# Which free slot a load takes: the one that has been free longest, in place of the lowest number

## The chip, the core and the metric

The kernel runs on one core of one Trainium2 chip. The metric is the device time of one execution in microseconds (us); lower is better. All data is in the chip's main memory (HBM) at the start and the result goes back there. The core has a matrix engine (PE, whose weight loads are listed apart as PEld), a vector engine (DVE), a scalar engine (ACT), GpSimd (POOL) and a sync engine (SP), which here issues all the kernel's transfers, one after another, in the order in which the program was written. Sixteen DMA engines carry the transfers out. Engines run unsynchronized and wait for one another on semaphores.

## The reference

Two layers of one-token decoding for a batch of eight, each an attention block over a key and value cache and a small mixer and feed-forward block. Both layers read the same weights and the same caches:

```
x = x + A(layernorm(x))      # attention, pass 1
x = x + B(layernorm(x))      # mixer + MLP
x = x + A(layernorm(x))      # attention, pass 2
x = x + B(layernorm(x))

A:  q = x @ wq                                  # D = 448, 16 query heads of 256
    scores = q . k_cache * 256**-0.5            # 8 kv heads, 4096 keys, Dh = 256
    out = (softmax(scores) @ v_cache) @ wo
B:  h = gelu(layernorm(x) @ w1); four shifted quarters of h; x1 = x + hs @ w2
    out = x1 + gelu(layernorm(x1) @ w3) @ w4
```

The sequence has one position, so every shift in B moves in zeros: the mixer's term vanishes, and w1 and w2 are never read. The caches are bfloat16: 8 batches x 8 kv heads x 4096 keys x 256, 2 MB for the keys and 2 MB for the values of one head of one batch. The values are read twice (once in each pass); most keys are read once and kept on the core between the passes, as told below.

## The kernel before

**Slots.** The on-core buffer for the caches is one array, `slab`, cut into `N_SLOTS = 31` slots of 512 KB (L480 and the lines before it hold their bookkeeping). A slot holds a quarter of one head's keys or values. Slots x and x+1 with even x are mates: a quarter and the next one of the same head can be loaded with a single 1 MB transfer into two mates ("a pair"); otherwise each quarter is a 512 KB transfer ("a single"). Slot 30 has no mate.

**Units and steps.** A unit is one kv head of one batch in one pass: `(p, b, g)`. The main loop goes over the units in a list, four steps for each unit, one for each quarter. In a step it calls `transposes` (DVE turns a raw quarter of the keys, 32 x 32 blocks, from the slot that it was loaded into, into another slot), `k_part` (PE: the scores of that quarter, L653) and one or more `v_part` (PE: probabilities times a quarter of the values, L630, some six steps later than the scores). When pass 1 of a batch is complete (`ends`), the small dense work follows on PE and DVE, spread over the steps up to `fence`: layer norms, the MLP and the next query. In that stretch PE also works through two heads of other batches so as not to stand still.

**What lives how long.** A slot with values is free after its `v_part`. A slot with raw keys is free after its two transposes (L562). A slot with transposed keys is free after `k_part` in pass 2; in pass 1 it stays occupied until pass 2 for six of the eight heads of a batch (`KEEP = 6`), two quarters of which are parked in PSUM instead. So by the end of pass 1 of a batch 22 of the 31 slots hold kept keys, and nine are left for everything in flight.

**The planner.** Which transfer goes into which slot is decided when the program is written, not on the chip: `free` is a Python list, to which a slot's number is appended by the code that writes its last reader. Each time something is freed, `pump` writes as many of the next loads as the list allows, and SP later waits, at each of them, until the slot's last reader has really finished. One slot is held back (`RESERVE = 1`), so that `transposes` always finds a destination. `take` gives a single slot: it prefers those whose mate isn't free, and of these the lowest number. `take_two` gives the lowest two free mates. Pairs are used only outside the dense stretches (`calm`), where loads are marked `wide`; where they are also `firm`, and seven or more quarters are under way, `pump` rather waits for two mates than write two singles. The planner's order of the loads themselves (`loads`), and the order of the work on PE, is fixed beforehand and does not look at slots.

Of the kernel before, what the change touches and what calls it, by code (L numbers as in the profile page):

```python
# [31 lines left out]
def kernel(  # L32
# [340 lines left out]
    lone = {b: [(1, b + 2, g) for g in loose] for b in range(4)}  # L373
# [102 lines left out]
    free = list(range(N_SLOTS))  # L476
# [3 lines left out]
    def take():  # L480

        lone = [x for x in free if x ^ 1 not in free]
        x = min(lone or free)
        free.remove(x)
        return x

    def take_two():

        both = [x for x in free if x % 2 == 0 and x + 1 in free]
        if both:  # L490
            free.remove(both[0])
            free.remove(both[0] + 1)
        return both[:1]
# [16 lines left out]
    def pump():  # L510
        while loads and len(free) > RESERVE:
            kind, t, i = loads[-1]
            _, b, g = units[t]
            if kind == "p":
                loads.pop()
                x = take()
                dst = slots[x].rearrange("p (e q c x) -> p q c e x", e=4, q=2, c=4)
                for j in range(2):
                    src = park[parked[g, i]][j][:].bitcast(BF16)
                    nc.scalar.copy(dst[:, j], src.rearrange("p (c e x) -> p c e x", c=4, e=4))  # L520
                kt_of[(1, b, g), i] = x
                continue
            cache, of = (A_k_cache, raw_of) if kind == "k" else (A_v_cache, v_of)
            n, two = 1, (kind, t, i + 1)
            if i % 2 == 0 and two in wide and two in loads[-PAIR_VIEW:]:
                x = take_two() if len(free) > RESERVE + 1 else []
                if x:
                    n, x = 2, x[0]
                    loads.remove(two)
                elif under_way[0] >= ENOUGH and two in firm:  # L530
                    return
            loads.pop()
            if n == 1:
                x = take()
# [14 lines left out]
    def transposes(i):  # L549


        while len(parts) - len(todo) < by[i]:
            t, s = todo[-1]
            if 4 * t + s > i and ((t, s) not in raw_of or not free):
                return
            todo.pop()
            raw = raw_of.pop((t, s))
            kt = kt_of[units[t], s] = take()
            src = slots[raw].bitcast(FP32).rearrange("p (q c e i) -> p q c e i", q=2, c=4, e=4)
            dst = slots[kt].bitcast(FP32).rearrange("p (e q c r) -> p q c e r", e=4, q=2, c=4)  # L560
            for q in range(2):
                nc.vector.transpose(dst[:, q], src[:, q])  # L562
            _, b, g = units[t]
            if (g, s) in parked:
                for q in range(2):
                    dst = park[parked[g, s]][q][:].rearrange("p (c e r) -> p c e r", c=4, e=4)
                    nc.vector.transpose(dst, src[:, q])
            free.append(raw)
            under_way[0] -= 1
            pump()  # L570
# [377 lines left out]
```

## Time and profile before

| | |
|---|---|
| median of three runs | 1114.25 us (1113.67 to 1115.25) |
| the profiled execution | 1115.99 us, of which 1114.2 us is the span from its first to its last instruction |
| busy share | PE 62%, PEld 58%, DVE 49%, ACT 27%, POOL 9% |
| moved by the DMA engines | 449.77 MB, mean 404 GB/s |
| loads into slots | 227 of 1024 KB, 378 of 512 KB |

The table says how long each engine was at work, not what the end waited for. A busy share is an average over stages with different limits: 62% of PE says nothing of the stretch in which PE is the one that holds up the rest. The rate of the DMA engines in a stretch is the measure that all stretches have in common here, since the bytes are nearly all of the same kind, loads into slots.

### The profile page before, as it was taken

What the parts mean: (1) busy time and instruction counts of PE and PEld (TensorE: products, weight loads), DVE (VectorE), ACT (ScalarE), POOL (GpSimd) and SP (SyncE); (2) the same over time, 40 slices, a digit from 0 to 9 for tenths busy, and PEclk for the clock granted to TensorE, in tenths of its full rate; (3) what the DMA queues carried; (4) which work ended last, traced back from release to release, by engine and by line L of the source; (5) the groups of instructions that cost most, each with busy time, mean ns of one, the idle gap of its engine ahead of it and who ended that gap; (6) DMA issues with size and microseconds to landing.
All of it is one profiled execution on the core that took longest, in us unless ns stands there. A gap on an engine that the chain in (4) does not pass through costs nothing.

```text
span 1114.2 us, 46349 instructions
## 1 busy us (share of the span) xinstructions
PE 687.9 (62%) x20737; PEld 640.8 (58%) x20737; DVE 550.7 (49%) x1305; ACT 306.0 (27%) x1360; POOL 104.1 (9%) x156
## 2 busy tenths in 40 slices
PE   3345675666756576565756667565756667665766
PEld 2334565565646565565655556565656566555765
DVE  4347554654446445554455535563446535554322
ACT  1112124321233212422243212422143212422242
POOL 0001001110011100110011000110011000100011
DMA  9999999999999999999999999999999999999993
GB/s 367 394 418 425 408 417 422 424 417 395 417 423 424 400 403 419 423 424 391 414 420 424 402 410 404 420 424 415 383 421 424 409 412 404 422 423 400 371 405 128
DMA packets 94503, 449.77 MB, mean 404 GB/s; under 512 B 9936, under 2 KB 15968, under 8 KB 64864
## 3 DMA queue, kind: packets, MB, share of 16 engines
q1 hardware_dynamic: 94304, 446.81, 98.4%
q8 instruction: 162, 2.65, 0.9%
q14 instruction: 37, 0.30, 0.1%
HBM read 446.77 MB, written 0.01 MB: 401 GB/s over the span
## 4 chain that ended last, share of the span: by engine, by line
DMA 39%; PE 15%; issue 6%; ACT 6%; DVE 5%; POOL 0%; SPq 0%; DVEq 0%; ACTq 0%; POOLq 0%
DMA slab<-in_A_v_cache_dram 31%; DMA slab<-in_A_k_cache_dram 9%; PE bank L630 5%; PE bank L653 4%; DVE slab L562 3%; ACT pt L720 2%; PE bank L137 1%; ACT slab L520 1%; ACT pe L689 1%; DVE small L686 1%; PE bank L676 1%; PE bank L712 1%; ACT pt_far L720 1%; PE bank L702 1%; PE bank L313 1%
## 5 line engine op out<-in xcount | busy, mean ns | idle before, releaser
L562 DVE STREAM_TRANSPOSE slab<-slab 128x512 f32<-128x512 f32 x640 | 414.6, 687 | 214.7 <-DMA slab<-in_A_k_cache_dram 167.2
L630 PEld LDWEIGHTS <-slab 128*128 128x128 bf16 x8192 | 273.1, 106 | 286.5 <-DMA slab<-in_A_v_cache_dram 223.0
L630 PE MATMUL bank<-pt,slab 128*128 128x2 bf16 x7168 | 260.5, 166 | 232.7 <-DMA slab<-in_A_v_cache_dram 161.5
L653 PE MATMUL bank<-Qblk,slab 128*128 128x8 bf16 x8192 | 297.2, 168 | 77.4 <-DVE slab L562 39.1
L653 PEld LDWEIGHTS <-slab 128*128 128x128 bf16 x8192 | 267.8, 105 | 88.2 <-DVE slab L562 46.6
L689 ACT ACTIVATE pe<-bank,small 128x32 bf16<-128x32 f32 x256 | 61.3, 295 | 406.7 <-DVE small L686 406.7
L731 POOL TENSOR_TENSOR small<-small 128x2 f32<-128x2 f32 x112 | 78.2, 698 | 773.2 <-DVE small L727 773.2
L720 ACT CAST pt<-bank 32x64 bf16<-32x64 f32 x448 | 90.8, 203 | 106.4 <-PE bank L712 102.5
L686 DVE TENSOR_REDUCE small<-bank 128x2 f32<-128x256 f32 x128 | 54.1, 423 | 103.2 <-PE bank L676 102.9
L727 DVE TENSOR_REDUCE small<-bank 128x2 f32<-128x64 f32 x128 | 27.1, 212 | 118.5 <-ACT pt L720 102.9
L166 ACT CAST Qblk<-bank 32x32 bf16<-32x32 f32 (+1 forms) x272 | 48.2, 177 | 110.7 <-PE bank L160 108.2
L676 PE MATMUL bank<-rows,small 128*128 128x128 bf16 x256 | 48.5, 293 | 11.5 <-DVE small L668 11.5
L668 DVE TENSOR_REDUCE small<-bank 128x2 bf16<-128x64 f32 x128 | 26.4, 206 | 58.5 <-PE bank L653 58.3
L630 PE MATMUL bank<-pt_far,slab 128*128 128x2 bf16 x1024 | 37.0, 166 | 26.1 <-DMA slab<-in_A_v_cache_dram 24.4
L712 PE MATMUL bank<-pe,rows 128*128 128x64 bf16 x512 | 51.3, 241 | 1.9 <-issue 1.9
L712 PEld LDWEIGHTS <-rows 128*128 128x128 bf16 x512 | 33.8, 124 | 28.4 <-issue 28.1
L702 PE MATMUL bank<-pe,small 128*128 128x64 bf16 x128 | 27.3, 213 | 30.7 <-ACT pe L689 29.4
L182 PEld LDWEIGHTS <-wo_sb 128*128 128x128 bf16 x1152 | 35.5, 104 | 8.8 <-issue 7.7
L182 PE MATMUL bank<-OT,wo_sb 128*128 128x1 bf16 x1024 | 33.2, 165 | 5.6 <-ACT OT L599 4.5
L137 PEld LDWEIGHTS <-wq_sb 128*128 128x128 bf16 x864 | 30.6, 106 | 10.3 <-issue 5.9
L520 ACT COPY slab<-park 128x1024 bf16<-128x1024 bf16 x32 | 30.1, 1029 | 9.4 <-DVE slab L562 9.3
L599 ACT ACTIVATE OT<-bank,small 128x2 bf16<-128x2 f32 x122 | 25.4, 261 | 24.1 <-PE bank L630 22.7
(113 smaller groups left out, 386.5 us busy)
## 6 DMA issues: line engine op xcount, KB each, us to landing
slab<-in_A_v_cache_dram SPq DMA_DIRECT2D x130, 1024.0 KB, 13.1
slab<-in_A_v_cache_dram SPq DMA_DIRECT2D x252, 512.0 KB, 8.1
slab<-in_A_k_cache_dram SPq DMA_DIRECT2D x97, 1024.0 KB, 14.0
slab<-in_A_k_cache_dram SPq DMA_DIRECT2D x126, 512.0 KB, 8.8
wo_sb<-in_A_wo_dram SPq DMA_DIRECT2D x4, 896.0 KB, 11.7
wq_sb<-in_A_wq_dram SPq DMA_DIRECT2D x3, 1024.0 KB, 6.8
w_sb<-in_B_w_dram SPq DMA_DIRECT2D x1, 1568.0 KB, 12.5
w_sb<-in_B_w_dram SPq DMA_DIRECT2D x3, 448.0 KB, 16.7
```

Of the source, the lines that this page charges most:

```text
L137: nc.tensor.matmul(pv[:, i, j, :], cols(big[:, c, :], m + i * half), rows[:, c, :], start=(i == 0 and j == 0 and c == 0), stop=True, skip_ ...
L166: nc.scalar.copy(dst, src)
L182: nc.tensor.matmul(y[:, c, :], chunk(wo_sb[:, k, :], c), o[:, k, :], start=False, stop=True, skip_group_check=True,)
L562: nc.vector.transpose(dst[:, q], src[:, q])
L630: nc.tensor.matmul(pos[t][:, k, :], vv[:, c, 128 * k : 128 * k + 128], pts[t][:, 8 * s + c, :], start=(t == 0 and s == 0 and c == 0 and k ...
L653: nc.tensor.matmul(scs[t][:, 2 * s + c, :, :], ktv[:, db, c, :, x], Qblk[run_of[t][0]][:, run_of[t][1], db, x, :, :], start=(db == 0 and x ...
L676: nc.tensor.matmul(mzs[t][:, 128 * h : 128 * h + 128], pm[:, h : h + 1].to_broadcast([128, 128]), ident, start=True, stop=True,)
L686: nc.vector.tensor_reduce(nm, mx, AX.X, ALU.max, negate=True)
L689: nc.scalar.activation(pe[:].rearrange("p c b h -> p h (c b)")[:, h], scs[t].rearrange("p c b h -> p h (c b)")[:, h], ACT.Exp, bias=nm[:, ...
L712: nc.tensor.matmul(pp[:, c], sel, pe[:], start=True, stop=True)
L720: nc.scalar.copy(pts[t][sl].rearrange("p (k c) h -> p k c h", c=4), pp[sl, :, :, pb, :].rearrange("p c k h -> p k c h"),)
L731: nc.gpsimd.tensor_tensor(out=rz_of[t], in0=zs, in1=mone, op=ALU.pow)
```

## The change

Both functions that choose slots use the order of the list `free` in place of the slot's number. The list is in the order in which the program freed the slots, so its first entry has been free longest. A single load, a transpose's destination or a copy back from PSUM takes the first entry of those it may take (as before, first those without a free mate). A pair is chosen by the later of its two halves: the pair whose younger half stands earliest in the list. How many slots are kept back, which loads may be pairs, and the order of the loads and of the work on the engines are as before.

```diff
     def take():
 
         lone = [x for x in free if x ^ 1 not in free]
-        x = min(lone or free)
+        x = (lone or free)[0]
         free.remove(x)
         return x
 
     def take_two():
 
         both = [x for x in free if x % 2 == 0 and x + 1 in free]
+        both.sort(key=lambda x: max(free.index(x), free.index(x + 1)))
         if both:
             free.remove(both[0])
             free.remove(both[0] + 1)
```

## The prediction

> **What bounds the kernel now.** I read the page's busy shares first, then its DMA queues, then its chain, then the rate by stage, and last SP's own waits.
>
> ```profile
> PE 687.9 (62%) x20737; PEld 640.8 (58%) x20737; DVE 550.7 (49%) x1305; ACT 306.0 (27%) x1360; POOL 104.1 (9%) x156
> ...
> q1 hardware_dynamic: 94304, 446.81, 98.4%
> ...
> DMA 39%; PE 15%; issue 6%; ACT 6%; DVE 5%; POOL 0%; SPq 0%; DVEq 0%; ACTq 0%; POOLq 0%
> ```
>
> No compute engine is full; the loads' queue holds the DMA engines 98.4% of the span, and the chain runs mostly through loads. So the time is bytes over rate, plus a start and a tail, and what counts is where the rate falls. The view by stages (the last two columns are the DMA engines' share, which counts overlapping packets and so can pass 1, and GB/s):
>
> ```profile
> 70.00:120.00 50.00, 29.95 (x773) 25.35 (x774) 36.15 (x71) 12.01 (x59) 4.18 (x6) 1.00 1.01 424
> ...
> 190.00:240.00 50.00, 32.08 (x982) 30.12 (x979) 30.76 (x65) 15.66 (x76) 5.58 (x8) 1.00 1.01 424
> 245.00:270.00 25.00, 16.77 (x498) 15.76 (x495) 10.57 (x32) 4.70 (x23) 2.09 (x3) 1.00 1.00 388
> 270.00:310.00 40.00, 26.97 (x827) 25.41 (x825) 20.38 (x48) 11.18 (x54) 4.04 (x6) 1.00 1.03 417
> 380.00:400.00 20.00, 12.43 (x360) 11.78 (x361) 8.25 (x24) 3.50 (x18) 2.01 (x3) 1.00 0.99 372
> 515.00:530.00 15.00, 9.43 (x270) 8.99 (x267) 5.28 (x17) 3.19 (x16) 0.70 (x1) 1.00 0.99 365
> 630.00:650.00 20.00, 12.84 (x412) 11.97 (x410) 9.60 (x20) 4.72 (x23) 1.39 (x2) 1.00 0.97 381
> 670.00:700.00 30.00, 20.37 (x644) 19.66 (x645) 16.09 (x37) 9.41 (x46) 3.34 (x5) 1.00 1.02 405
> 770.00:810.00 40.00, 26.50 (x810) 25.33 (x810) 15.88 (x50) 8.11 (x39) 2.82 (x5) 1.00 1.01 391
> 880.00:900.00 20.00, 12.09 (x366) 11.42 (x366) 9.34 (x19) 5.58 (x28) 2.09 (x3) 1.00 1.00 397
> 915.00:940.00 25.00, 18.60 (x571) 17.67 (x568) 13.31 (x34) 7.59 (x36) 2.65 (x4) 1.00 1.02 401
> 1000.00:1020.00 20.00, 12.56 (x387) 11.46 (x384) 8.55 (x18) 5.11 (x24) 2.09 (x3) 1.00 1.00 393
> 1030.00:1050.00 20.00, 16.00 (x506) 15.46 (x506) 7.88 (x32) 4.05 (x19) 1.94 (x3) 1.00 0.99 376
> 1050.00:1070.00 20.00, 12.95 (x400) 12.30 (x398) 6.53 (x16) 9.73 (x34) 2.10 (x3) 1.00 0.99 371
> 1070.00:1090.00 20.00, 13.25 (x431) 12.67 (x429) 6.03 (x14) 5.84 (x28) 2.09 (x3) 1.00 1.01 424
> 1090.00:1114.20 24.20, 14.90 (x440) 13.90 (x437) 6.22 (x28) 4.31 (x20) 4.70 (x5) 1.00 0.20 83
> ```
>
> A stretch of pairs runs at 424, an undisturbed stretch of singles at 417. Against 417, a stretch of t us at g GB/s has lost t x (1 - g/417). Two kinds of dip stand out. The first lies in and just after the dense stretches, where all loads are singles: 1.7 us lost at 245, 2.2 at 380, 1.9 at 515, 0.9 at 670, 2.5 at 770, 1.0 at 915, 2.0 at 1030, together 12. The second lies where the pairs end: 1.7 at 630, 1.0 at 880, 1.2 at 1000, 2.2 at 1050, together 6. These 18 us are what slots can win or double; the start (first 70 us) and the tail without loads (some 20 us) have other causes.
>
> SP's waits show who opens the way for a load, and a timeline of SP how a dip of the first kind looks:
>
> ```profile
> SPq L536 <- PE bank L630: 202.2, 174, 5.0
> SPq L536 <- DVE slab L562: 97.6, 49, 6.0
> SPq L536 <- PE bank L653: 81.2, 64, 8.3
> ```
>
> ```profile
> 789.17 5.50 SPq L536 DMA_DIRECT2D slab<-in_A_k_cache_dram  x4
> 798.02 0.33 SPq L536 DMA_DIRECT2D slab<-in_A_v_cache_dram  x1
> ```
>
> SP stands before nearly every load until the slot's last reader is done. From 794.7 to 798.0 it issues nothing, since PE does the dense matmuls of L137 and empties no slot. Setting the planner's list beside the trace (each slot's release is the end of the last matmul or transpose of the step that frees it): all through 788 to 802 us slot 29, empty since 787.6, is held back, and ten loads in a row take the slot emptied last, because its number is lower. At 798.0 two singles are left in flight, under 3 us of work.
>
> **The change, part by part.**
>
> *Singles take the older slot.* Over the whole kernel as it is, 445 of the 714 single takes pass over an older slot; for 232 of the 378 single loads that older slot had been emptied over 0.3 us earlier. With the change each of these loads waits for the release before the one it waits for now, so one more single is in flight: 0.524 MB at 417 GB/s, 1.26 us of work for the DMA engines. That is worth nothing while the queue is deep, and up to 1.26 us at each dip of the first kind. 770 to 810 holds two dips, so eight dips give at most 10.1 us, and no dip gives more than it lost (0.9 and 1.0 are less), which cuts this to 9.4. At the least it is 0: at 380 to 400 hardly over a third of the loads (6 of 15) had an older slot. I take two thirds, the share of single loads that had an older slot being 232/378 = 0.61: **-6 us**, between 0 and -9.4.
>
> *Lone slots go to transposes by age.* In the pair stretches a lone slot that has been idle long has a mate with kept keys. Lowest number leaves such slots lying (30 has no mate; 29 and 23 also lay 10 us and longer; at 1006 us three had lain since 942, 975 and 991) and breaks mates that were about to come free together. By age the idle ones are filled with kept keys, so raw keys leave whole pairs and the firm rule waits less. This bears on the second kind of dip: before 636 us SP issued one pair in 11 us while four lone slots lay free. At most all 6 us go; at worst the new arrangement holds pairs back longer and the 6 double. I take half of the gain, since the fragments named are of the kind that age clears first: **-3 us**, between -6 and +6.
>
> *More pairs, fewer singles.* Only nine loads in the calm part were written as singles after a pair had been looked for, so the counts hardly move; a pair for two singles saves 1.049 MB x (1/417 - 1/424) = 0.04 us. Nothing either way (under 0.4 us).
>
> *Transposes take the younger slot.* The held-back slot is now always the one freed last, and it is the transpose's destination. In the dense stretches DVE then waits for PE's last `v_part` where it used to find a slot long empty: at 797.7 it wrote into slot 29 at once. What queues behind it on DVE is the maximum of the scores (L668), on which PE's softmax matmuls wait, and behind the transposes the raw slot and `k_part`.
>
> ```profile
> DVE slab L562 <- PE bank L630: 40.4, 25, 4.6
> ...
> PEld L653 <- DVE slab L562: 46.6, 62, 5.5
> ```
>
> One such wait is 40.4/25 = 1.6 us, one of PE for a transpose 46.6/62 = 0.75 us. The least is 0 (DVE is 49% busy, and most of its transposes wait for their own keys anyway: 167.2 us for L562 by the page's groups). The most is one full wait in every dense stretch and one behind its fence, 16 x 1.6 = 26 us. I take one PE wait of 0.75 us in half of those 16 places, plus none hidden: 6, of which half passes on, as the DMA queue holds three to five singles there (4 to 6 us): **+3 us**, nearer to 0 for that cover.
>
> No instruction is added or removed; the same bytes are moved; SP's order of loads is the same. SP passes each load earlier, and no other work is in its queue. ACT and POOL have no slot work but the 16 copies from PSUM, which sit well behind their data.
>
> Sum: -6 - 3 + 3 = -6 us. The profiled execution took 1115.99 us (span 1114.2 and 1.8 around it), 1.7 over the median; it would become 1110, and the median 1114.25 becomes **1108**.
>
> **The rivals.**
>
> *Transposes are held up (slower).* Place: the held-back slot in and behind the dense stretches. DVE runs its queue in order, so a transpose that waits for the youngest slot also delays the softmax, and late raw slots delay loads. For: loads and transposes share the same nine slots, and what one gains in lead the other gives up; after a fence PE is at 80% and more (1030 to 1050: 16.0 of 20 us). Against: the trace shows these transposes well ahead of their use. It decides once more than 9 us of the 26 reach the end; at half, 13 us against 9 of gain, the time is 1118. If the second kind of dip doubled as well, 1125 is the far end.
>
> *Hidden anyway (no change).* The loads in a dip are gated by PE; a queue that starts one single deeper drains as low a little later, and the lead is used up without being refilled. For: at 380 the release times were almost in order already. Also the list's order is the program's, not the chip's: where DVE runs late, the first entry isn't the first empty. Then 0 to -2 us: 1113. The Trainium skill speaks for this case too: its page "DMA: Bandwidth & Descriptors", section Specifications, puts the HBM limit for one core at about 358 GB/s, by which a core at 404 has nothing left to win and the time stays at 1114. The trace doesn't agree: 424 GB/s is held for 50 us at a time.
>
> *Everything fits (much faster).* All 18 us of dips go and no wait comes: 1096. For it speaks only that one idle slot is seen in both kinds; against, that PE sets the pace at 1030 to 1050.
>
> **How the numbers follow.** Forecast (1103 to 1111.9): 0.50. Much faster (below 1103): 0.12. Hidden (1112 to 1116.5): 0.15. Held up (over 1116.5): 0.23. A measurement of this kernel tells about 0.2%, 2.2 us. Faster takes the first two, 0.62; the hidden case is the middle, 0.15; slower 0.23. The range from 1100 to 1121 leaves out about 0.06 below (half of the much faster case) and 0.1 above.
>
> **What would show it.** Right: SP issues through 794 to 798; DMA in the first kind of dip at 400 GB/s or more; SP's waits at L536 less bunched. The second part: no SP pause as at 624 to 636. Wrong: more DVE time waiting at L562 for L630 than 40 us, PE waiting for L562 far over 46.6 and 39.1 us, or new stretches under 390 GB/s in the calm part.

## The result, and the profile after

| | before | changed |
|---|---|---|
| median of nine runs | 1114.25 us (1113.67 to 1116.6) | 1118.23 us (1116.4 to 1119.84) |
| profiled execution | 1115.99 us, span 1114.2 | 1116.4 us, span 1114.6 |
| ratio of the times | | 1.003, 95% interval 1.002 to 1.0041 |

The change makes the kernel 0.3% slower. The prediction was 1108, 6 us faster, in a range of 1100 to 1121 which holds the time; its direction was wrong. The time is that of the rival "transposes are held up" (1118), to which it gave 0.23.

The profile shown of the changed kernel is its fastest run of the nine, level with the execution shown of before; a second profile of the same program, at 1118.2 us, is used below to tell lasting differences from chance. All lines of the code past the diff are one higher: L630 is now L631, L653 is L654, L562 is L563.

First the queue, the chain and the loads of the changed kernel's page:

```profile
q1 hardware_dynamic: 94304, 446.81, 98.3%
...
DMA 60%; PE 17%; ACT 7%; DVE 7%; issue 7%; SPq 1%; POOL 1%; DVEq 0%; ACTq 0%; POOLq 0%
...
slab<-in_A_v_cache_dram SPq DMA_DIRECT2D x133, 1024.0 KB, 12.4
slab<-in_A_v_cache_dram SPq DMA_DIRECT2D x246, 512.0 KB, 8.6
slab<-in_A_k_cache_dram SPq DMA_DIRECT2D x94, 1024.0 KB, 13.2
slab<-in_A_k_cache_dram SPq DMA_DIRECT2D x132, 512.0 KB, 9.2
```

The loads still set the pace. Keys and values have traded a few pairs, but there are 227 pairs and 378 singles, just as before. Now the stages, the same columns as in the prediction (the last two are the DMA engines' share and GB/s):

```profile
70.00:120.00 50.00, 29.47 (x763) 24.98 (x764) 36.24 (x70) 12.01 (x58) 4.19 (x6) 1.00 1.01 423
...
245.00:270.00 25.00, 16.79 (x494) 15.66 (x491) 10.58 (x32) 4.71 (x23) 2.10 (x3) 1.00 1.01 395
...
380.00:400.00 20.00, 12.21 (x351) 11.60 (x352) 8.28 (x24) 3.52 (x18) 1.74 (x3) 1.00 0.98 361
515.00:530.00 15.00, 9.73 (x280) 9.30 (x278) 5.52 (x17) 3.17 (x16) 0.70 (x1) 1.00 0.99 374
630.00:650.00 20.00, 12.50 (x404) 12.02 (x405) 8.60 (x19) 4.50 (x22) 1.40 (x2) 1.00 1.00 409
650.00:670.00 20.00, 13.29 (x407) 12.61 (x407) 6.59 (x27) 3.07 (x16) 1.40 (x2) 1.00 1.02 393
670.00:700.00 30.00, 20.61 (x641) 19.76 (x638) 15.72 (x37) 9.57 (x46) 3.36 (x5) 1.00 1.02 402
770.00:810.00 40.00, 28.22 (x866) 26.99 (x865) 17.38 (x53) 8.82 (x43) 3.82 (x6) 1.00 1.00 392
810.00:820.00 10.00, 7.09 (x218) 6.52 (x215) 5.45 (x12) 2.62 (x13) 0.70 (x1) 1.00 1.02 395
880.00:900.00 20.00, 11.68 (x361) 11.05 (x362) 9.47 (x20) 5.91 (x28) 2.10 (x3) 1.00 1.01 417
915.00:940.00 25.00, 17.21 (x529) 16.51 (x527) 12.06 (x31) 7.13 (x34) 2.65 (x4) 1.00 0.99 381
1000.00:1020.00 20.00, 12.67 (x400) 12.08 (x398) 8.75 (x19) 5.54 (x27) 1.71 (x3) 1.00 1.01 419
1030.00:1050.00 20.00, 14.93 (x459) 14.25 (x459) 6.16 (x29) 4.03 (x19) 1.94 (x3) 1.00 1.01 397
1050.00:1070.00 20.00, 14.32 (x451) 13.66 (x448) 7.57 (x18) 9.52 (x35) 2.11 (x3) 1.00 0.93 350
```

With the prediction's own measure, t x (1 - g/417), the dips where pairs end are nearly gone at 630, 880 and 1000 (0.4 us lost in place of 3.8). But the dips in and behind the dense stretches are as deep as before: 12.1 us in place of 12. And there are new losses: 1.2 us from 650 to 670, at the start of a dense stretch, 0.5 from 810 to 820, behind its fence, and 3.2 in place of 2.2 from 1050, behind the last fence. (The prediction counted this last stretch among the ends of the pair stretches; by the matmuls of the planner's steps its fence is passed at 1047.) The kernel before, in these stretches and in the one from 790:

```profile
650.00:660.00 10.00, 5.48 (x162) 5.10 (x160) 1.86 (x6) 2.18 (x12) 0.70 (x1) 1.00 1.02 417
660.00:670.00 10.00, 8.04 (x240) 7.66 (x241) 5.02 (x21) 0.76 (x4) 0.70 (x1) 1.00 1.03 418
...
790.00:800.00 10.00, 7.86 (x241) 7.68 (x241) 3.98 (x15) 2.75 (x14) 1.25 (x2) 1.00 1.02 399
...
810.00:820.00 10.00, 6.90 (x222) 6.56 (x220) 6.00 (x13) 2.90 (x14) 1.22 (x2) 1.00 1.03 416
```

So part of what looks mended has only moved on. From 630 to 670 the loss was 1.7 us and is 1.5; what 880 gained, 1.0, the stretch from 915 lost, where the loss went from 1.0 to 2.2. Near 800 the sign that the prediction had named for being right did show: SP issues loads between 794 and 798.

```profile
796.81 0.33 SPq L537 DMA_DIRECT2D slab<-in_A_k_cache_dram  x1
797.24 0.37 SPq L537 DMA_DIRECT2D slab<-in_A_v_cache_dram  x1
```

```profile
790.00:800.00 10.00, 8.32 (x253) 7.99 (x250) 2.18 (x14) 3.34 (x16) 1.25 (x2) 1.00 1.03 417
800.00:810.00 10.00, 6.36 (x207) 6.13 (x208) 6.66 (x13) 2.27 (x11) 0.70 (x1) 1.00 0.98 373
```

The ten microseconds from 790 rose from 399 to 417 GB/s, but those from 810 fell from 416 to 395, and 770 to 810 as a whole stands at 392 in place of 391. In the second profile 810 and 1050 are worse still (358 and 338), which is most of its 1.8 us more.

What has changed most is whom SP and DVE wait for. SP's own waits in the changed kernel, and DVE's at the transposes (waited for, us in total, times, longest):

```profile
SPq L537 <- PE bank L631: 190.3, 172, 4.1
SPq L537 <- DVE slab L563: 182.4, 89, 6.5
...
SPq L537 <- PE bank L654: 39.3, 38, 4.9
```

```profile
DVE slab L563 <- PE bank L654: 40.0, 13, 5.1
...
DVE slab L563 <- PE bank L631: 4.0, 9, 1.2
```

SP's waits for transposes rose from 97.6 to 182.4 us, while those for PE's scores and values fell from 283 to 230. DVE's waits at the transposes for the values' matmuls fell from 40.4 to 4.0 us, and in their place it waits 40.0 us for the scores', 2.0 before. The second profile has 181.1 and 40.2.

Two places show what this looks like. SP's timeline of the changed kernel behind the last fence with a line of DVE's there, and then DVE's behind the fence near 800 us:

```profile
1052.69 8.78 SPq L537 DMA_DIRECT2D slab<-in_A_v_cache_dram  x3
1061.52 0.43 SPq L537 DMA_DIRECT2D slab<-in_A_k_cache_dram  x1
```

```profile
1059.78 1.30 DVE L563 STREAM_TRANSPOSE slab<-slab 128x512 f32<-128x512 f32 x2
```

```profile
801.69 3.83 DVE L563 STREAM_TRANSPOSE slab<-slab 128x512 f32<-128x512 f32 x6 [5.14 <-PE bank L654]
```

In the first, the last of the three loads is a pair, issued at 1061 us; the load before it went out at 1054. One of its two slots held raw keys, which DVE transposed only at 1059.8 to 1061.1, behind the softmax work in its queue. The list then also held single slots that PE had left at 1056, but the loads that take them stand later in SP's queue. (This load is a pair, and its two mates were the only whole pair in the list; the singles are counted below.) In the second, DVE idles 5.1 us before the first transpose behind the fence, since that transpose's destination is the slot which the first scores have just emptied; before, slot 29 lay ready there. This happens once in each of the eight batches.

### The profile page after: what moved, and what is told of

Same layout as the page of the kernel before. It is cut to its first block, busy times and chain, and to the rows that moved or that the text cites. A ratio compares the mean times of both kernels' runs of the same rounds, so it can differ in the third digit from the quotient of the medians.

```text
span 1114.6 us, 46351 instructions
## 1 busy us (share of the span) xinstructions
PE 687.2 (62%) x20737; PEld 640.8 (57%) x20737; DVE 550.8 (49%) x1305; ACT 306.7 (28%) x1360; POOL 104.4 (9%) x156
## 3 DMA queue, kind: packets, MB, share of 16 engines
q1 hardware_dynamic: 94304, 446.81, 98.3%
## 4 chain that ended last, share of the span: by engine, by line
DMA 60%; PE 17%; ACT 7%; DVE 7%; issue 7%; SPq 1%; POOL 1%; DVEq 0%; ACTq 0%; POOLq 0%
DMA slab<-in_A_v_cache_dram 45%; DMA slab<-in_A_k_cache_dram 14%; PE bank L631 6%; DVE slab L563 4%; PE bank L654 4%; ACT pt L721 2%; ACT slab L521 2%; PE bank L137 2%; PE bank L677 1%; SPq L537 1%; DVE small L687 1%; ACT pe L690 1%; ACT pt_far L721 1%; DMA wq_tl<-in_A_wq_dram 1%; PE bank L713 1%
## 5 line engine op out<-in xcount | busy, mean ns | idle before, releaser
L563 DVE STREAM_TRANSPOSE slab<-slab 128x512 f32<-128x512 f32 x640 | 414.1, 687 | 219.2 <-DMA slab<-in_A_k_cache_dram 168.3
L631 PEld LDWEIGHTS <-slab 128*128 128x128 bf16 x8192 | 272.7, 106 | 277.6 <-DMA slab<-in_A_v_cache_dram 222.3
L631 PE MATMUL bank<-pt,slab 128*128 128x2 bf16 x7168 | 259.7, 166 | 226.1 <-DMA slab<-in_A_v_cache_dram 166.8
L654 PE MATMUL bank<-Qblk,slab 128*128 128x8 bf16 x8192 | 297.9, 168 | 76.3 <-DVE slab L563 39.1
L654 PEld LDWEIGHTS <-slab 128*128 128x128 bf16 x8192 | 268.1, 105 | 85.6 <-DVE slab L563 46.5
L631 PE MATMUL bank<-pt_far,slab 128*128 128x2 bf16 x1024 | 37.0, 166 | 25.6 <-DMA slab<-in_A_v_cache_dram 24.6
```

Of the source, the lines that this page charges most:

```text
L631: nc.tensor.matmul(pos[t][:, k, :], vv[:, c, 128 * k : 128 * k + 128], pts[t][:, 8 * s + c, :], start=(t == 0 and s == 0 and c == 0 and k ...
L654: nc.tensor.matmul(scs[t][:, 2 * s + c, :, :], ktv[:, db, c, :, x], Qblk[run_of[t][0]][:, run_of[t][1], db, x, :, :], start=(db == 0 and x ...
```

## The experiments

Each kernel is compared with the kernel before on the same chip. In the edits, `take` is given a rule for each of its three callers, single loads, transposes and copies from PSUM (here against the changed kernel; e9 to e12 and e16 add further rules):

```diff
-    def take():
+    def take(rule):
 
-        lone = [x for x in free if x ^ 1 not in free]
-        x = (lone or free)[0]
+        c = [x for x in free if x ^ 1 not in free] or free
+        x = min(c) if rule == "low" else c[-1] if rule == "young" else c[0]
```

| run | single loads | transposes | pairs | median us | ratio to before (95%) |
|---|---|---|---|---|---|
| e1 | age | lowest | lowest | 1118.91 | 1.0034 (1.0021 to 1.0048) |
| e2 | lowest | age | lowest | 1113.44 | 0.9994 (0.9983 to 1.0006) |
| e18 = e2 again | lowest | age | lowest | 1114.22 | 0.9991 (0.9982 to 1.0001) |
| e3 | lowest | lowest | age | 1115.76 | 1.0004 (0.9996 to 1.0012) |
| e4 | youngest | age | age | 1114.58 | 0.9997 (0.9988 to 1.0005) |
| e8 = the change again | age | age | age | 1118.01 | 1.0033 (1.002 to 1.0046) |
| e5 | age, youngest before the fence | age | age | 1116.35 | 1.0018 (1.0007 to 1.0029) |
| e6 | lowest, age before the fence | lowest | lowest | 1116.79 | 1.0017 (1.0005 to 1.003) |
| e7 | age, two slots held back | age | age | 1120.37 | 1.0055 (1.0042 to 1.0068) |
| e9 | age, late raw slots last | age | age | 1115.22 | 1.0003 (0.9995 to 1.0012) |
| e10 | as e9, youngest before the fence | age | age | 1115.06 | 0.9999 (0.999 to 1.0008) |
| e11 | lowest, raw slots first | lowest | lowest | 1117.52 | 1.0019 (1.001 to 1.0029) |
| e12 | lowest, raw slots last | lowest | lowest | 1118.31 | 1.0025 (1.0015 to 1.0035) |
| e13 | age in pair stretches only | same | same | 1115.96 | 1.0007 (0.9997 to 1.0018) |
| e14 | age in dense stretches only | same | same | 1120.16 | 1.0055 (1.0035 to 1.0075) |
| e15 | lowest | age | age | 1116.37 | 1.0014 (1.0004 to 1.0023) |
| e16 | lowest, raw slots last | age | lowest | 1115.02 | 1.0004 (0.9993 to 1.0016) |
| e17 | lowest, youngest before the fence | age | lowest | 1115.33 | 1.0001 (0.999 to 1.0012) |

### Which part of the change

**Single loads by age alone (e1)**, against the kernel before:

```diff
-            if n == 1:
-                x = take()
+            if n == 1:
+                x = take("old")
```

> Only the single loads take the oldest free slot; transposes, copies and pairs take the lowest number as before. Theory H (in the dense stretches loads and transposes share one held-back slot: a load that takes the older one leaves the transpose the younger one, or waits itself for a transpose that comes late): the dense dips are as deep as in the changed kernel and the gain at the ends of the pair stretches is absent, so about 1118 to 1121, slower than both. Rival G (the lead of the loads is worth what the prediction said, and the loss sits with the transposes' or the pairs' rule): 1108 to 1111. Rival L (the times of all arrangements scatter by some 4 us and the rule means nothing): 1112 to 1119, with no relation between this run's profile by stages and those of the two kernels.

1.0034: this part alone brings a loss as large as the change's, and with it the same kind of waits; DVE waits 40.8 us for the scores at its transposes, SP 155.1 for transposes. The prediction's chief gain is the loss.

**Transposes by age alone (e2, and again as e18)**:

```diff
-            kt = kt_of[units[t], s] = take()
+            kt = kt_of[units[t], s] = take("old")
```

> Only the transposes take the oldest free slot; loads, copies and pairs the lowest number. Theory H: the pair stretches end without the pause of SP (419, 417 and 409 GB/s at 630, 880 and 1000 in place of 381 to 397, worth some 3 us), and the dense dips are those of the kernel before: 1110 to 1112. Rival G: the loss is here, 1116 to 1120. Rival L: 1112 to 1119.

> The same program as the run with the transposes by age alone: 0.06% under the kernel before if that was real, so 1113.5 to 1115 beside a kernel before at 1115; within 0.2% of it in any case.

0.9994 and 0.9991. Both lie under 1 by 0.7 to 1 us, both intervals take in 1. It isn't a loss, and as a gain it isn't settled. SP's waits for transposes are 121.9 us here, more than the 97.6 of before, at no cost that shows.

**Pairs by age alone (e3)**, with only the line `both.sort(...)` of the change:

> Only the choice among whole free pairs goes by age; singles, transposes and copies take the lowest number. All theories but L: after the first 70 us there are rarely two whole pairs to choose from, so nothing changes, 1113.5 to 1115. Rival L: anything from 1112 to 1119.

1.0004: nothing, as all theories but one had it.

**Singles take the youngest slot (e4)**, against the changed kernel:

```diff
             if n == 1:
-                x = take()
+                x = take("young")
```

> As the changed kernel, but single loads take the slot freed last, so that the oldest stays held back for the transposes. Theory H: the transposes find their destination empty, raw keys come free earlier, and the dense dips are shallower than with singles by age: the gain at the ends of the pair stretches stays and the dense stretches cost no more than before, 1109 to 1113. Theory of the prediction (lead of the loads fills the dips): one single less in flight at every dip, 6 us lost, 1120 to 1124. Rival L: 1112 to 1119.

0.9997, where the prediction's theory asked for 1120 to 1124. Singles now take the slot that was freed last, and nothing is lost. The waits of DVE for the scores are gone too (1.2 us), and SP's for transposes are down to 78.2. So letting singles take the older slot gains nothing that can be measured here, and something about it has a price. What a whole single more in flight would be worth this run doesn't tell: at their issue, singles found as many quarters under way as in the kernel before (within 0.1).

### The wait behind the fence

**Youngest slot for the singles just before each fence (e5)**, those of the last seven steps (eleven by the planner's lists; the expectation says ten), so that the first transpose behind it finds a slot emptied six steps earlier. `now[0]` is the step of the main loop:

```diff
+    near = {4 * f + k for f in fence for k in range(-6, 1)}
...
-                x = take()
+                x = take("young" if now[0] in near else "old")
```

> As the changed kernel, but the ten single loads written between the last transpose of a dense stretch and the first one behind its fence take the youngest slot, so that this first transpose (once in each batch) finds a slot emptied six steps earlier. Theory H1 (what costs is that this one transpose stands behind the first scores after the fence, 3 to 4 us on DVE, and with it the raw key slots): the waits of DVE for the scores' matmuls at the transposes (40 us, 13 times) fall below 10 us, and the time to 1111 to 1114. Theory of the lead (single loads by age are worth something, the loss lies elsewhere): the lead is lost just where the queue is shallowest, 1119 to 1122. Rival S (singles by age cost because SP, in order, stands at raw slots all through the dense stretches, not only at the fence): the waits go but the time stays, 1116 to 1119.

**The same singles by age in the kernel before (e6)**: `take("old" if now[0] in near else "low")`, all else by lowest number.

> As the kernel before, but those ten single loads of each batch take the oldest slot, so that the first transpose behind the fence gets the slot that the first scores have just emptied. Theory H1: this alone brings the loss, 1117 to 1120, with the 3 to 4 us waits of DVE at the transposes. Theory of the lead: 1110 to 1113. Rival S: near the kernel before, 1114 to 1116.

By the medians e5 takes away about half of the loss and e6 makes about half of it. The loss in e6 is clear of zero; the gain of e5 over the change isn't, since their intervals overlap (1.0007 to 1.0029, 1.002 to 1.0046 for e8). DVE's waits moved as meant: 12.1 us at seven transposes in e5, and in e6

```profile
DVE slab L564 <- PE bank L655: 42.2, 11, 5.5
DVE slab L564 <- PE bank L632: 31.1, 17, 4.6
```

e6 has the full 40 us of DVE's waits and only 1.9 us of loss, with SP waiting 96.8 us for transposes, no more than before. So the fence's wait has a price without SP's waits growing, but it is not the whole story, and rival S (SP stands at raw slots) is left.

**Two slots held back in the dense stretches (e7)**:

```diff
-        while loads and len(free) > RESERVE:
+        while loads and len(free) > RESERVE + (not calm[max(now[0], 0) // 4]):
```

> As the changed kernel, but two slots are held back in place of one while the dense work runs, so the transposes get a slot that is one release older and each load a slot one release younger. Theory H1: the transpose behind the fence takes a slot that values left in the step before, PE has passed it, so most of the DVE wait goes: 1112 to 1115. Theory of the lead: one single less in flight in each dip, 1121 to 1124. Rival S: between, 1116 to 1120.

DVE's waits for the scores fell to 9.1 us, but the time rose to 1120.37, against theory H1. SP still waits 172.9 us for transposes. So a slot taken out of use costs more than the waits it saves. That would fit a queue whose depth has some worth; no run prices the depth alone.

**The changed kernel again (e8)** beside these runs:

> The changed kernel itself, for times and a second profile beside these runs: 1117 to 1119, with the DVE waits for the scores at the transposes again about 40 us in 13 times, since the same program has the same slots.

1118.01, with the same slots and the same waits.

### Raw slots

In the changed kernel 124 of the 378 singles go into a raw key slot, nearly all (112) in the very step whose transposes free it; before it was 80. (These and the other counts of slots are read off the planner's lists.)

**Late raw slots last (e9)**: among the candidates a single passes over a raw slot freed less than four steps ago. **The same with the youngest slot before the fence (e10).**

```diff
+        late = [x for x in c if now[0] - was_raw.get(x, -9) < 4]
+        if rule == "old but late":
+            x = ([x for x in c if x not in late] or c)[0]
```

> As the changed kernel, but single loads pass over a raw key slot freed less than four steps ago as long as another is there (22 raw slots go to single loads then, against 116 in the kernel with singles alone by age). The first transpose behind each fence still gets the slot that the first scores have just emptied. Theory two costs (of the 3 to 4 us, about half is the transpose's wait behind the fence, half is SP standing in order at raw slots whose transposes come late): SP's waits for transposes fall from 182 us to about 100, and the time to 1115.5 to 1117. Theory H1 alone (only the fence): 1117.5 to 1119. Theory of the lead (the older slot is the better one for a load): 1119 or more.

> As the run before it, and the ten single loads before each fence take the youngest slot, so that both costs are gone and the age rule stays for transposes and pairs. Two costs: 1113 to 1115, at or a little under the kernel before. H1 alone: like the kernel with only the fence mended, 1116 to 1117. Lead: 1120 or more.

1.0003 and 0.9999: the loss is gone in both. SP and DVE in e9:

```profile
SPq L543 <- DVE slab L569: 71.7, 33, 4.2
```

```profile
DVE slab L569 <- PE bank L662: 40.2, 9, 6.7
```

DVE still waits its 40 us behind the fences, and here that costs nothing that can be measured, with hardly any load behind the late transposes. The four kernels with all else by age make a square:

| | raw slots taken by age | late raw slots passed over |
|---|---|---|
| fence's wait kept | 1.0030 and 1.0033 | 1.0003 |
| fence's wait mended | 1.0018 | 0.9999 |

In this square the raw slots are worth 0.2 to 0.3%; the fence's wait is worth 0.1% where singles go into raw slots, which isn't clear of the intervals, and nothing seen where they don't. The square doesn't hold all else fixed. The slots chosen also change how many pairs get written: 227 in the changed kernel, 231 in e5 and e10, 234 in e9. By the prediction's 0.04 us for a pair, seven of them are 0.3 us, a tenth of the difference, and the kernel before has 227 too and no loss; but no run varies the pairs alone.

**Raw slots first (e11) and last (e12) in the kernel before**, by lowest number within each kind:

```diff
+        raws = [x for x in c if x in was_raw]
+        if rule == "raw first":
+            x = min(raws or c)
+        elif rule == "raw last":
+            x = min([x for x in c if x not in was_raw] or c)
```

> The kernel before, but a single load takes a raw key slot first whenever one is among its candidates (116 of 378 in the step in which it was freed, against 80 raw slots in all before); the transpose behind the fence keeps an old slot, and nothing goes by age. Two costs: the raw half of the loss alone, 1116 to 1118, with SP waiting longer for transposes than the 98 us of before. H1 alone: 1114 to 1115.5.

> The kernel before, but a single load takes a raw key slot only when nothing else is there, so nearly all go into slots that PE has just emptied. Two costs: SP's waits for transposes fall below 98 us and the time is that of before or a little better, 1113 to 1115. H1 alone: 1114 to 1115.5. Lead (the younger slot costs 1.26 us at each dip): 1118 to 1122.

e11 came as expected: 121 singles in raw slots, no first transpose behind a fence in the slot that the scores have just left, SP waiting 157.4 us for transposes, 1.0019. e12 is a miss: SP's waits for transposes fell to 80.7 us and the time rose to 1.0025 all the same. Only the theory of the lead had asked for that.

### Dense or pair stretches

**Age in one kind of stretch only**: `take("old" if calm[max(now[0], 0) // 4] else "low")` at all three callers, and pairs sorted likewise (e13); the condition turned round (e14).

> Age for every choice in the pair stretches, lowest number in the dense ones. Theory D (the loss is made in the dense stretches): 1113 to 1115, no slower than the kernel before. Theory C (it is made in the pair stretches, by lone slots that lie idle): this list has 2.83 free slots on average there, against 3.22 before and 3.52 with the change, so faster than before, 1111 to 1113.5. Both fall if it is 1117 or more.

> Age for every choice in the dense stretches, lowest number in the pair ones. Theory D: the loss is here, 1117 to 1120. Theory C: 2.91 free slots on average in the pair stretches, so no slower than before, 1113 to 1115.

Age in the pair stretches alone makes no difference that the runs can tell, age in the dense stretches alone costs 0.55%. So it is the choices in the dense stretches that cost. The count of free slots lying in the pair stretches, which theory C made the cause, does not order these two (2.83 and 2.91).

**The change without its singles' part (e15)**, and **the miss with the transposes by age (e16)**:

> The change without its singles' part: transposes, copies and pairs by age, single loads by lowest number. Theories D and C both (2.88 free slots in the pair stretches): 1112 to 1114.5, with DVE waiting for the scores at its transposes in only part of the batches. If 1116 or more, the parts do not add and the arrangement as a whole decides.

> The kernel that missed (a single load takes a raw slot only when nothing else is there, 3.33 free slots in the pair stretches, 1118.3), now with the transposes by age (3.08). Theory C: the miss came from the pair stretches, so 1114 to 1116. Lead (loads into the slot emptied last cost by themselves): 1117 to 1119 again.

e15 is a miss: at 1116.37 (1.0014) it lies in the range that its expectation had kept for "the parts do not add". It is better than the change by about half its loss, but not as good as e2, from which it differs in the pairs' and the copies' rule. In two of the eight batches its first transpose behind the fence gets the slot that the scores have just left; e2's never does there. e16 is at 1.0004: singles take slots by the same rule as in e12, and nothing is lost. So the singles' rule of e12 does not lose by itself; the loss came with the lowest number for the transposes. In e12 the singles of the dense stretches found 4.9 quarters under way at their issue, in e16 and before 5.2 (counted from the issues and completions of the traces), so less was in flight there in e12. What made it so no run shows, and the lead as e12's price isn't ruled out.

**e2 with the fence mended (e17)**:

> Transposes by age, all else by lowest number, and the ten single loads before each fence take the youngest slot. If the loss lies with the dense stretches alone: 1112.5 to 1114.5. If the free slots lying in the pair stretches count (3.30 here, 2.99 without the mend): 1115 to 1117.

1.0001 (1115.33 beside 1115.37 for the kernel before): no better than e2. The median lies in the range given to the free slots in the pair stretches, but its interval takes in e2's two values, and e2 had little to mend: DVE waits 7.3 us for the scores there and 8.0 here. No arrangement tried is faster than the kernel before beyond its interval.

**All kernels side by side.** SP's waits for transposes part the runs well. In the eight profiles in which they come to 130 us or more (the change, e8, e1, e5, e7, e11, e14, e15) every kernel is slower than before with its interval clear of 1. Of the eleven at 125 us or less (e2, e18, e3, e4, e6, e9, e10, e12, e13, e16, e17) nine are level. The two that lose are e6, which has the fence's wait, and e12. This is an ordering found afterwards; it says where the losses go together with SP's waits, not that nothing else differs.

## Why the prediction was wrong

**What bounds the kernel: right.** The loads still hold the DMA engines 98.3% of the span, and the dips were rightly named, but for the one from 1050, which lies behind a fence. The ends of the pair stretches ran faster where the prediction looked for it, and the loss turned up in part a stretch later.

**"Singles take the older slot", -6 us: this step failed.** Alone it measured +3.8 us (0.34% of 1115). Three things were wrong in it. First, "one more single is in flight" did not come about. The slots are a fixed number, and what the loads gain the transposes give up: by one and the same count from issues and completions, singles found only some 0.2 quarters more under way at their issue than before, and a single key quarter stood some 0.6 us longer from its landing to the end of its transpose. Second, a dip that starts later is not a dip filled: near 800 SP issued through the pause that the prediction had seen, and the loss came 20 us later. That is the mechanism of the rival "hidden anyway". Third, the term has no place for what the older slot is waiting for. The list's order is the order in which the program frees slots, over two engines. A raw slot is listed when its transposes are written; PE's next releases come later in the list but sooner in time, whenever DVE is behind. Of the 104 singles that SP issued just as a raw slot became free, 82 stood there while another slot of the list was empty already, 59 us in all; before it was 43 of 63, 39 us (planner's lists set beside the two traces). The prediction had this as half a sentence in "hidden anyway" and gave it no price.

These counts alone do not prove the price. At slots that PE empties it is the other way round: before, 201 of 230 singles stood while another slot was empty, 147 us, and with the change none of 113 did. The change did what it was meant to do there, and the time got no better. That the waits at raw slots are the ones that cost rests on the edits: e9 and e10, which pass over late raw slots, lose nothing, and e11, which seeks raw slots, loses 0.19%.

The trace agrees here with the Trainium skill's page "DMA: Bandwidth & Descriptors", section "Anatomy of one DMA — SWDGE (gpsimd) path": a DMA's semaphore wait is held by the sequencer that issues it, before it is handed to the DMA engines. In this kernel that sequencer is SP, and one load that waits 6.5 us for a transpose keeps back all loads behind it.

**"Lone slots go to transposes by age", -3 us: the sign may be right, the size was not.** The dips at 630, 880 and 1000 shrank by 3.4 us in the changed kernel's profile, in part by moving on, and alone the rule came to -0.06 and -0.09%, 0.7 and 1 us, not clear of zero.

**"More pairs, fewer singles", nothing: right.** 227 and 378 in both.

**"Transposes take the younger slot", +3 us: near in size, wrong in the way.** e6 made 1.9 us of it and e5 took back 1.7. The prediction had DVE wait for the last values' matmuls and delay the softmax. DVE in fact waits for the first scores behind the fence, and its idle time before transposes is hardly longer in sum (219.2 us, 214.7 before). Of the signs named for being wrong, those of the waits did not show: DVE's waits for the values fell to 4.0 us, and PE's waits for transposes stayed at 46.5 and 39.1. New stretches under 390 GB/s in the calm part did, behind two fences: 930 to 940 fell from 404 to 380, 1060 to 1070 from 392 to 319. In e9 40 us of DVE's new waits had no cost that can be measured, in e6 42 us cost 0.17%; what makes the difference is not shown. SP, the next in line behind a late raw slot, is the likely one in the changed kernel.

**The sum.** In ratios, +0.34% for singles, -0.08% for transposes (the mean of e2 and e18) and +0.04% for pairs make +0.30%, 3.3 us, and 1.003 was measured. That this sum closes is luck: e15, all of the change but its singles, measured +0.14%, where the same terms make -0.04%. The rival of 1118 had the right place, the held-back slot in and behind the dense stretches, and named late raw slots among its ways; but it took its price from DVE's waits and from 9 us of gain that never came, so that its time fits is luck as well. What stays open is why e12 lost 0.25% and e15 0.14%: the arrangement of slots as a whole has an effect of that size that none of the accounts foretells.

## What to carry to other kernels

An order written down by the planner is the order of the program, and slots come free in the order of the engines; where one in-order queue waits for slots that several engines release, "freed longest ago" by the list can be the slot that is ready last. Before giving a resource's lead to one user, name who had it: with a fixed number of slots, a load that goes out earlier leaves a transpose a later slot. And the sum of an engine's waits is not their price: 40 us on DVE went with a loss in the changed kernel and in e6, and with none in e9.

## What the runs showed that was not expected

Nothing new of the chip itself. Of the measurement: one and the same program spread over 1112.2 to 1118.5 us in 33 runs beside each other, so a profile of a single execution can tell no difference of 3 us, as the pair shown above (1115.99 and 1116.4 for medians 4 us apart) bears out; the sums of waits, which were the same to some 2 us in the two profiles of the changed kernel (the three lines shown of SP's and the two of DVE's), were the better guide.
